# One load in place of three for the last rows of W_down, and seven loads in place of five for x, in a decode block

## Chip, core and metric

The kernel runs on one core of one Trainium2 chip. The metric is device time in microseconds (us), as the median of several runs. The core has five engines that run side by side and wait for each other on semaphores: PE (TensorE, matrix products), DVE (VectorE), ACT (ScalarE), POOL (GpSimd) and SP (SyncE, which here only issues loads). Sixteen DMA engines bring data from the chip's memory (HBM) into the core's SBUF, 128 partitions of on-chip memory. A load is issued by SP or ACT, is cut into packets that the sixteen engines share out, and tells its end by a semaphore.

## What is computed

One decoding step of a transformer block for two sequences (B = 2), one token each, in bf16: layer norm, attention over a cache of 8192 positions and 32 heads, a residual, a second layer norm, and a gated feed-forward part.

```python
x = A_x                                              # (2, 1, 512)
q = layernorm(x) @ wq                                # 512 -> 32 heads x 128
p = softmax(q . k_cache * 128 ** -0.5)               # k_cache, v_cache: (2, 32, 8192, 128)
h = x + (p @ v_cache) @ wo                           # 4096 -> 512
n = layernorm(h)
h2 = h + (relu(n @ W_gate) * (n @ W_up)) @ W_down    # 512 -> 1376 -> 512
```

The two caches make up 256 MiB of the 281 MB that are read; everything else is small beside them.

## The kernel before

**Tiles.** Three buffers of 128 x 32768 bf16 (8 MB each, `bufs[0]` to `bufs[2]`) hold what is streamed from HBM. A step works on four heads of one sequence and needs one K tile and one V tile of 8 MB. There are 15 such steps (0 to 14, `Q` = 14 is the last) and two half steps of two heads each at the end. K and V tiles alternate over the three buffers, so at any time one tile is worked on while others are on their way. Below, K0 is the K tile of step 0, V1 the V tile of step 1, and so on.

**A step.** `products` (line 375) multiplies the K tile by the repeated q on VectorE, in place; `scores` (lines 393 to 399) sums the products by halving and ends in `scol`, the scores. A part of the columns goes through PE instead (`scores_pe`). Then come the largest score, the exponentials on ACT, and `values` (line 446), where PE multiplies them with the V tile. A K buffer is free when `scores` has ended on VectorE, and a V buffer when `values` has ended on PE; the next tile for the buffer is issued by SP (`load_tile`, line 165) once these have told it so. The order on every engine is the order of the program text, written out by hand.

**The head.** ACT issues x (line 190) in five pieces, one row at a time: 512 B, 512 B, 512 B, 256 B and 256 B. SP issues wq (line 193, 4 MB), K0 and V0. x, wq and the row form of q share the third buffer, so K1, which is to go there, waits until q has been made. From x follow its transposition (lines 238 and 239), the layer norm (`ln_cols`), q (line 252), its spreading over the partitions (lines 259 to 271), its transposition (line 275) and the copies `qTs` (line 276), after which VectorE begins step 0.

**The tail.** When attention nears its end, SP issues wo in pieces, then W_gate and W_up (line 612) and W_down (lines 616 and 621). W_down has 1376 rows, which are 10 chunks of 128 and one of 96. The last chunk is kept as 128 partitions that begin 32 rows early, at row 1248 (`FSETS[-1]`), because W_gate and W_up are read in the same 128 columns: partitions 0 to 31 of chunk 10 (`FC - 1`) repeat rows that chunk 9 has. So that they count once, line 616 loads only partitions 32 to 127, as three loads of 32 rows of 1 KB, and line 647 sets the 32 others to zero on VectorE. The other chunks follow in four loads (line 621): chunks 0 to 4, 5 to 7, 8, and 9. The end of the kernel is `g_ps` = n W_gate, `gate` = relu(g) times a factor (line 706), `u_ps` = n W_up, `hm` = gate times u (line 727) in two parts, and `down` (line 719), which takes chunks 0 to 4, then chunk 10, then 5 to 9. The sums are copied to `yrow` (lines 734 and 735), and line 736 writes it out.

**Completion semaphores.** The loads of SP and ACT share eight completion semaphores, given out in turn in the order of the program text. A load waits until the load eight places before it, which had the same semaphore, is complete. In the built program before, x has numbers 0 to 4, wq 5, K0 6, V0 7, and none of these waits; K1 is the next with number 0. At the tail, the three small loads of W_down wait for the V tile of the last half step and for two pieces of wo, the following ones for further pieces of wo, the last one (chunk 9) for W_gate, and the write of the result for W_up.

Of the kernel before, what the change touches and what calls it, by code (L numbers as in the profile page):

```python
# [13 lines left out]
def _free(t, offset, dims):  # L14

    return bass.AP(tensor=t.tensor, offset=t.offset + offset, ap=[t.ap[0]] + [list(d) for d in dims])


def _dram(t, offset, dims):
    return bass.AP(tensor=t.tensor, offset=t.offset + offset, ap=[list(d) for d in dims])  # L20
# [3 lines left out]
def kernel(  # L24
# [13 lines left out]
    nc = tc.nc  # L38
    P = nc.NUM_PARTITIONS
    B, Sq, D = A_x.shape  # L40
    _, Hkv, Sk, Dh = A_k_cache.shape
    Hq = A_wq.shape[1] // Dh
    F = B_W_gate.shape[1]
# [29 lines left out]
    FSETS = [(0, 5), (5 * P, 3), (8 * P, 1), (9 * P, 1), (F - P, 1)]  # L73
    FC = 11
    AGAIN = 32
# [51 lines left out]
    wd_sb = bufs[1][:, 0:FC * D].rearrange("p (c n) -> p c n", c=FC)  # L127
# [58 lines left out]

    with tc.manual_schedule():

        for b, k, n in ((0, 0, 2), (0, 2, 2), (1, 0, 2), (1, 2, 1), (1, 3, 1)):
            nc.scalar.dma_start(  # L190
                out=xr[b:b + 1, k * P:(k + n) * P], in_=_dram(A_x, b * D + k * P, [[D, 1], [1, n * P]]),
            )
# [9 lines left out]
            out=nscale, in_=nscale, compare_op=ALU.not_equal, fill=-SCALE,  # L202
# [5 lines left out]
            out=ident_f, in_=ident_f, compare_op=ALU.not_equal, fill=1.0,  # L208
# [4 lines left out]
            out=sel, in_=sel, compare_op=ALU.not_equal, fill=1.0,  # L213
# [9 lines left out]
            out=pick, in_=pick, compare_op=ALU.not_equal, fill=1.0,  # L223
# [24 lines left out]
        for g0 in range(0, NQ, 4):  # L248
            for n0 in range(NH * g0 * Dh, NH * (g0 + 4) * Dh, 4 * Dh):
                q_ps = ps2.tile([B, 4 * Dh], f32, tag="o")  # L250
                for c in range(KC):
                    nc.tensor.matmul(  # L252
                        out=q_ps, lhsT=xn[:, c, :], rhs=wq_sb[:, c, n0:n0 + 4 * Dh], start=(c == 0), stop=(c == KC - 1),
                    )
                nc.vector.tensor_copy(qrow[:, n0:n0 + 4 * Dh], q_ps)
            for b in range(B):
                r_ps = ps2.tile([P, 4, Dh], f32, tag="tp")
                for j in range(NH):
                    nc.tensor.matmul(
                        out=r_ps[j * (P // NH):(j + 1) * (P // NH)], lhsT=sel[:, b, 0:P // NH],  # L260
# [5 lines left out]
        for j in range(2):  # L266
            nc.tensor.matmul(
                out=r_ps[j * (P // 2):(j + 1) * (P // 2)], lhsT=sel[:, B - 1, :],
# [38 lines left out]
        def sums(i):  # L307

            _, _, n, z = heads(i)
            z_ps[i] = ps.tile([P, n], f32, tag="mx", name="z_ps")  # L310
            nc.tensor.matmul(out=z_ps[i], lhsT=ones, rhs=z, start=True, stop=True)
# [175 lines left out]
        def lay_rows(k, sps, scalar=False):  # L487

            r = SROWS[k]
            or_ps = ps.tile([P, B, r], f32, tag="mx")  # L490
            for b in range(B):
                nc.tensor.matmul(out=or_ps[:, b, :], lhsT=sps[b], rhs=rest[r], start=True, stop=True)
            if scalar:
                nc.scalar.activation(out=orow[k], in_=or_ps.rearrange("p b c -> p c b"), func=ACT.Copy)
            else:
                nc.vector.tensor_copy(orow[k], or_ps.rearrange("p b c -> p c b"))
# [90 lines left out]
        for k in range(1, len(SETS)):  # L587
# [3 lines left out]
            out=wo[:, (HM + 1) * D:Hq * D], in_=_dram(A_wo, (HM + 1) * Dh * D, [[P // 4 * D, 4], [D, P // 4], [1, D]]),  # L591
# [19 lines left out]
        for w, src in ((0, B_W_gate), (1, B_W_up)):  # L611
            nc.sync.dma_start(
                out=wgu[:, w].rearrange("p c f -> p (c f)"), in_=_dram(src, 0, [[KC * F, P], [1, KC * F]]),
            )
        for q0 in range(AGAIN, P, AGAIN):
            nc.sync.dma_start(
                out=wd_sb[q0:q0 + AGAIN, FC - 1, :], in_=_dram(B_W_down, (F - P + q0) * D, [[D, AGAIN], [1, D]]),
            )
        for f0, n in FSETS[:-1]:
            fc = f0 // P  # L620
            nc.sync.dma_start(out=wd_sb[:, fc:fc + n, :], in_=_dram(B_W_down, f0 * D, [[n * D, P], [1, n * D]]))
        late = bufs[1][:, HALF + D:HALF + D + P + D]
        hrow, parts3 = late[0:3 * B, 0:D], late[0:3 * B, D:D + B]
# [6 lines left out]
            out=z2_ps, lhsT=ones, rhs=_free(zc, ((B - 1) * NQ + groups[Q][1]) * NH, [[1, nb]]), start=True, stop=True,  # L630
# [13 lines left out]
        values_cols(p1, 0, half)  # L644
        for k in range(1, len(SETS)):
            lay_rows(k, sps[k - 1])
        nc.vector.memset(wd_sb[0:AGAIN, FC - 1, :], 0.0)
        sums(Q + 2)
        shares(Q + 2)
        values_cols(p1, half, p1.nt)  # L650
# [43 lines left out]
        for c in range(KC):  # L694
            nc.tensor.transpose(hT_ps[:, c, :], hb[:, c].rearrange("p k b -> p (k b)"), ident)
        nc.scalar.activation(
            out=hrow.rearrange("q (p c) -> q p c", c=KC), in_=hT_ps.rearrange("q c p -> q p c"), func=ACT.Copy,
# [7 lines left out]
        gate = small.tile([P, FC, B], f32, tag="gate")  # L705
        nc.vector.scalar_tensor_tensor(
            out=gate, in0=g_ps, scalar=0.0, in1=_free(rvar, 0, [[0, FC], [1, B]]), op0=ALU.max, op1=ALU.mult,
        )
        parts = [(range(0, UP), "of", ps), (range(UP, FC), "tp", ps2)]
        u_ps = [pool.tile([P, len(part), B], f32, tag=tag, name="u_ps") for part, tag, pool in parts]  # L710
        SIDE = P // KC
# [55 lines left out]
```

## Time and profile before

| | |
|---|---|
| runs, median (lowest to highest) | 659.28 us (658.91 to 659.56, 3 runs) |
| the profiled execution: span from the first to the last instruction | 657.5 us |
| HBM read, rate over the span | 281.05 MB, 427 GB/s |
| busy: VectorE, PE, ACT, POOL | 85%, 54%, 19%, 4% |
| mean granted TensorE clock | 0.76 |
| chain that ended last: DMA, VectorE, PE | 37%, 42%, 18% |
| the loads of x in that chain | 2.0% |
| VectorE idle before line 375, waiting for a K tile | 44.9 us in 13 waits |

The page of a profile sums up one execution. Its chain follows the work that ended last back to the start, at each step to what released it. A timeline lists instructions by their start, with the length, the engine, the line, what is written and read, and in brackets the time that the engine was idle before and what ended that. SPq and ACTq are the issues of loads by SP and ACT. Windows give the busy time of each engine in a stretch of time. An engine that is busy is not for that reason the one that sets the time: VectorE is busy for 85% of the span and still waits for K tiles.

### The profile page before, as it was taken

How to read it: one execution, taken by the hardware profiler on the slowest of the kernel's cores; microseconds unless marked ns; L12 is line 12 of the kernel's file. 1: busy time of each engine (PE TensorE's matmuls, PEld its weight loads, DVE VectorE, ACT ScalarE, POOL GpSimd, SP SyncE). 2: the span in 40 equal slices, each digit the busy share in tenths (PEclk: the TensorE clock that was granted, in tenths of full speed). 3: DMA queues.
4: the chain of work that ended last, by engine and by line, in shares of the span. 5: the costliest groups of instructions: out<-in, count | busy, mean ns of one | idle time of the engine just before them, and what ended most of it. 6: DMA issues, size and time to landing. Idle time of an engine off the chain costs nothing.

```text
span 657.5 us, 5117 instructions
## 1 busy us (share of the span) xinstructions
PE 352.1 (54%) x2118; PEld 158.9 (24%) x2118; DVE 558.1 (85%) x252; ACT 123.6 (19%) x337; POOL 24.1 (4%) x36
## 2 busy tenths in 40 slices
PE   0730934809175380926539092552918458291997
PEld 0310311304022130312204031220403224030456
DVE  0599697988979799897979989796997969999982
ACT  0230030200203020030301103030210304201870
POOL 3080000000000000000000000000000000000020
PEclk9975775958778596877959687695968869686895
DMA  9999999999999999999999999999999999999997
GB/s 383 447 444 447 387 440 443 447 399 444 439 443 436 419 436 435 439 439 436 423 443 424 439 440 427 447 416 443 439 423 440 423 443 436 423 444 413 425 425 291
DMA packets 6948, 281.37 MB, mean 428 GB/s; under 512 B 809, under 2 KB 1422, under 8 KB 1934
## 3 DMA queue, kind: packets, MB, share of 16 engines
q1 hardware_dynamic: 6916, 281.06, 99.1%
q8 instruction: 16, 0.26, 0.1%
q14 instruction: 6, 0.05, 0.0%
q10 hardware_dynamic: 10, 0.00, 0.0%
HBM read 281.05 MB, written 0.00 MB: 427 GB/s over the span
## 4 chain that ended last, share of the span: by engine, by line
DVE 42%; DMA 37%; PE 18%; ACT 1%; issue 1%; ACTq 0%; SPq 0%; DVEq 0%
DMA tile<-in_A_k_cache_dram 30%; DVE tile L375 19%; DVE tile L393 18%; PE pv_ps L446 16%; DMA tile<-in_A_wo_dram 4%; DVE scol L395 2%; DMA tile<-in_A_x_dram 2%; DMA tile<-in_B_W_down_dram 1%; PE q_ps L252 1%; DVE pgq L420 1%; ACT ecol L415 1%; DVE pm L399 1%; DVE qrep L395 0%; DVE pm L410 0%; DVE hmax L412 0%
## 5 line engine op out<-in xcount | busy, mean ns | idle before, releaser
L446 PE MATMUL pv_ps<-tile,pgq 128*16 128x512 bf16 x960 | 244.3, 421 | 235.8 <-DVE pgq L420 223.2
L375 DVE TENSOR_TENSOR tile<-tile,qrep 128x29696 bf16<-128x29696 bf16 (+3 forms) x16 | 232.4, 14524 | 44.9 <-DMA tile<-in_A_k_cache_dram 44.9
L393 DVE TENSOR_TENSOR tile<-tile 128x14848 bf16<-128x14848 bf16 (+7 forms) x68 | 236.4, 3477 | 2.2
L446 PEld LDWEIGHTS <-pgq 128*16 128x16 bf16 x960 | 91.6, 97 | 378.1 <-DVE pgq L420 234.5
L451 ACT ACTIVATE pv<-pv_ps 16x512 f32<-16x512 f32 (+1 forms) x16 | 9.4, 589 | 243.7 <-PE pv_ps L446 243.6
L350 ACT ACTIVATE tile<-t_ps 128x1024 bf16<-128x1024 bf16 x53 | 52.6, 1022 | 12.6 <-PE t_ps L349 12.1
L415 ACT ACTIVATE ecol<-scol,nmax 128x256 bf16<-128x256 f32 x14 | 7.1, 508 | 196.1 <-DVE nmax L414 196.1
L340 PE MATMUL row_ps<-tile,qz 128*24 128x512 bf16 (+1 forms) x98 | 30.1, 389 | 18.0 <-ACT tile L350 17.9
L349 PE MATMUL t_ps<-ident,tile 128*128 128x128 bf16 x424 | 32.3, 229 | 13.0 <-DMA tile<-in_A_k_cache_dram 13.0
L349 PEld LDWEIGHTS <-tile 128*128 128x128 bf16 x424 | 25.8, 103 | 28.1 <-issue 14.2
L395 DVE TENSOR_REDUCE scol<-tile 128x232 f32<-128x1856 bf16 (+1 forms) x14 | 28.9, 2067 | 0.5
L641 POOL TENSOR_TENSOR tile<-ident 6x2 bf16<-6x2 bf16 x1 | 2.1, 2147 | 583.5 <-ACT tile L381 583.5
L420 DVE TENSOR_TENSOR pgq<-ecol,ownb 128x1024 bf16<-128x1024 bf16 x15 | 10.4, 692 | 10.3 <-ACT ecol L415 10.3
L381 ACT ACTIVATE tile<-tile 128x128 bf16<-128x128 bf16 x60 | 17.6, 293 | 1.9 <-DVE tile L375 1.9
L281 POOL COPY qzp<-qTs 128x4 bf16<-128x4 bf16 x1 | 15.0, 14982 | 26.1 <-DVE qTs L276 26.1
L375 DVE TENSOR_TENSOR tile<-tile,qpair 128x4096 bf16<-128x4096 bf16 (+3 forms) x4 | 15.5, 3883 | 0.0
L340 PEld LDWEIGHTS <-qz 128*24 128x24 bf16 (+1 forms) x98 | 7.9, 92 | 27.6 <-issue 22.7
L239 DVE CAST xc<-x_ps 128x8 f32<-128x8 bf16 x1 | 0.2, 167 | 15.5 <-PE x_ps L238 15.5
L367 ACT ACTIVATE scol<-sc_ps 32x24 f32<-32x24 f32 (+1 forms) x56 | 11.7, 209 | 7.7 <-PE sc_ps L362 7.2
L362 PE MATMUL sc_ps<-ident_f,tile 24*128 24x24 f32 (+2 forms) x68 | 7.2, 220 | 11.1 <-ACT tile L358 11.1
L358 ACT ACTIVATE tile<-row_ps 24x512 f32<-24x512 f32 (+2 forms) x17 | 10.0, 586 | 13.5 <-PE row_ps L340 13.5
L381 ACT ACTIVATION_READ_ACCUMULATOR tile<-tile 128x1 f32 x60 | 11.2, 186 | 0.0
(133 smaller groups left out, 143.8 us busy)
## 6 DMA issues: line engine op xcount, KB each, us to landing
tile<-in_A_k_cache_dram SPq DMA_DIRECT2D x2, 4096.0 KB
tile<-in_A_v_cache_dram SPq DMA_DIRECT2D x2, 4096.0 KB, 19.6
tile<-in_A_wq_dram SPq DMA_DIRECT2D x1, 4096.0 KB, 12.2
tile<-in_A_wo_dram SPq DMA_DIRECT2D x1, 2048.0 KB
tile<-in_B_W_gate_dram SPq DMA_DIRECT2D x1, 1376.0 KB, 22.8
tile<-in_B_W_up_dram SPq DMA_DIRECT2D x1, 1376.0 KB
tile<-in_A_wo_dram SPq DMA_DIRECT2D x1, 1024.0 KB, 23.8
tile<-in_B_W_down_dram SPq DMA_DIRECT2D x1, 640.0 KB
```

What stands on the lines that cost most here:

```text
L281: nc.gpsimd.tensor_copy(qzp[:, :, 6:8], qTs[:, B - 1, Hq - NH:Hq].rearrange("p (k j) -> p k j", j=2),)
L340: nc.tensor.matmul(out=row_ps, lhsT=z, rhs=s.kt[:, (nv + c0 + k) * Dh:(nv + c0 + k + 4) * Dh], start=(u == 0), stop=(u == U - 1),)
L349: nc.tensor.transpose(t_ps[:, k, :], s.kt[:, t * Dh:(t + 1) * Dh], ident)
L350: nc.scalar.activation(out=s.kt[:, (nv + c0) * Dh:(nv + c0 + TPC) * Dh], in_=t_ps.rearrange("p t s -> p (t s)"), func=ACT.Copy,)
L367: nc.scalar.activation(out=scols[s.i][r, nv:s.nt].rearrange("p (u t) -> p t u", t=4), in_=sc_ps[r, :, :, j], func=ACT.Copy,)
L375: nc.vector.tensor_tensor(out=kv, in0=kv, in1=_free(s.qr, 0, [[0, n], [1, Dh]]), op=ALU.mult)
L381: nc.scalar.activation(out=kv, in_=kv, func=ACT.Copy, accum_out=scols[s.i][:, t:t + 1])
L393: nc.vector.tensor_tensor(out=lo, in0=lo, in1=hi, op=ALU.add)
L395: nc.vector.tensor_reduce(out=scol[:, s.na:s.nv], in_=_free(s.kt, s.na * Dh, [[Dh, s.nv - s.na], [1, 8]]), axis=AXIS.X, op=ALU.add,)
L415: nc.scalar.activation(out=ecol, in_=scols[s.i], func=ACT.Exp, scale=SCALE, bias=nmax, accum_out=zs[:, s.b, s.g:s.g + 1],)
L420: nc.vector.tensor_tensor(out=s.pg, in0=_free(ecol, 0, [[VG, s.nt // VG], [0, NH], [1, VG]]), in1=_free(ownb, 0, [[0, s.nt // VG], [VG, NH ...
L446: nc.tensor.matmul(out=pv_ps[s.i][r, :], lhsT=s.pg[:, u].rearrange("p j t -> p (j t)"), rhs=s.vt[:, u * VG * Dh:(u + 1) * VG * Dh], start= ...
```

## The change

W_down's last chunk is loaded whole, all 128 partitions with one load, so that partitions 0 to 31 hold rows 1248 to 1279 a second time; this load goes ahead of the four others, where the three small ones stood. The zeroing of these partitions of W_down on VectorE goes, and the same 32 partitions of `gate` are zeroed for chunk 10 after `gate` is made, so that `hm` is zero there. x comes in seven loads: 512 B and six times 256 B.

```diff
-        for b, k, n in ((0, 0, 2), (0, 2, 2), (1, 0, 2), (1, 2, 1), (1, 3, 1)):
+        for b, k, n in ((0, 0, 2), (0, 2, 1), (0, 3, 1), (1, 0, 1), (1, 1, 1), (1, 2, 1), (1, 3, 1)):
             nc.scalar.dma_start(
                 out=xr[b:b + 1, k * P:(k + n) * P], in_=_dram(A_x, b * D + k * P, [[D, 1], [1, n * P]]),
             )
...
-        for q0 in range(AGAIN, P, AGAIN):
-            nc.sync.dma_start(
-                out=wd_sb[q0:q0 + AGAIN, FC - 1, :], in_=_dram(B_W_down, (F - P + q0) * D, [[D, AGAIN], [1, D]]),
-            )
-        for f0, n in FSETS[:-1]:
-            fc = f0 // P
+        for f0, n in FSETS[-1:] + FSETS[:-1]:
+            fc = min(-(-f0 // P), FC - 1)
             nc.sync.dma_start(out=wd_sb[:, fc:fc + n, :], in_=_dram(B_W_down, f0 * D, [[n * D, P], [1, n * D]]))
...
-        nc.vector.memset(wd_sb[0:AGAIN, FC - 1, :], 0.0)
...
+        nc.vector.memset(gate[0:AGAIN, FC - 1, :], 0.0)
```

The number of transfers is the same, 56 with the write of the result. Between x and W_down each load has a semaphore two places further on: x has 0 to 6, wq 7, K0 0 and V0 1. In the built program K0 therefore waits for the first load of x and V0 for the second.

## The prediction

> **What bounds the kernel now.** I read the page first (busy shares, slices, queues), then the chain that ended last, then SyncE's and VectorE's timelines, then the last microseconds in windows.
>
> ```profile
> DMA  9999999999999999999999999999999999999997
> ...
> q1 hardware_dynamic: 6916, 281.06, 99.1%
> ...
> q10 hardware_dynamic: 10, 0.00, 0.0%
> ```
>
> The DMA engines work in every slice but the last. Queue q1 (SyncE's loads) holds 99.1% of the time of 16 engines; so a microsecond in which the engines have nothing to fetch is a microsecond lost, and a computation counts only if it makes a load late. Queue q10 holds the five loads of x: ten packets, two a load.
>
> In the chain of waits (start, length, what):
>
> ```profile
> 2.11 12.96 DMA tile<-in_A_x_dram
> 15.07 0.14 issue
> ...
> 30.63 0.31 PE r_ps L267 x2
> 30.96 41.50 DMA tile<-in_A_k_cache_dram
> 72.48 15.64 DVE tile L375
> ```
>
> x, 2 KB, lands only at 15.07 us, and the whole making of q hangs on it until the third tile load (K of step 1) goes out at 30.96. SyncE's issues (start, length):
>
> ```profile
> 0.74 0.39 SPq L193 DMA_DIRECT2D tile<-in_A_wq_dram  x1
> 1.19 0.41 SPq L165 DMA_DIRECT2D tile<-in_A_k_cache_dram  x1
> 1.66 0.42 SPq L165 DMA_DIRECT2D tile<-in_A_v_cache_dram  x1
> 30.96 0.33 SPq L165 DMA_DIRECT2D tile<-in_A_k_cache_dram  x1
> 64.47 0.33 SPq L165 DMA_DIRECT2D tile<-in_A_v_cache_dram  x1
> 83.93 0.33 SPq L165 DMA_DIRECT2D tile<-in_A_k_cache_dram  x1
> ```
>
> Wq, K0 and V0 go out at once; V1 (64.47) waits for VectorE to finish step 0's scores, which free K0's buffer, and K2 (83.93) for PE's values of step 0. VectorE's timeline:
>
> ```profile
> 32.31 0.19 DVE L276 COPY qTs<-qT_ps 128x32 bf16<-128x32 bf16 x1 [0.35 <-PE qT_ps L275]
> 32.41 15.08 DVE L375 TENSOR_TENSOR tile<-tile,qrep 128x28672 bf16<-128x28672 bf16 x1
> ...
> 62.30 2.02 DVE L395 TENSOR_REDUCE scol<-tile 128x224 f32<-128x1792 bf16 x1
> ...
> 72.48 15.62 DVE L375 TENSOR_TENSOR tile<-tile,qrep 128x29696 bf16<-128x29696 bf16 x1 [5.49 <-DMA tile<-in_A_k_cache_dram]
> ```
>
> Step 0's products begin 0.10 us after q is ready, without idle time, and step 0 runs through to the end of scol; after step 0 VectorE idles 5.49 us. So a later q moves V1's issue one for one, and what counts is how far ahead of need V1 is issued.
>
> **The change, part by part.** *x by seven loads.* The page does not say where x's 13 us go; the trace's records of single packets on q10 do:
>
> ```
> load   data at   bytes   completion at
> x0      1.64      512        1.66
> x1      6.17      512        7.40
> x2      8.62      512        9.85
> x3     11.07      256       12.29
> x4     12.30      256       14.73
> ```
>
> All of x goes through one engine (the spacing shows it). There each of x1's to x4's packets, the 4-byte completion too, waits for its turn behind one packet of q1: 1.22 us apart while these are Wq's 32 KB rows, 2.43 us for the last, behind a 64 KB row of K0 (2.42 us in q1's records). x0 alone went through before Wq's first packet (1.78). Two more loads are four more packets, all after Wq's end (its completions lie at 12.00 to 12.62) and within K0's (31.32 to 31.94): 4 x 2.43 = 9.7 us. x lands at 24.8. ACT's two more issues (0.21 to 0.27 us each) lie under this.
>
> What follows at the other stations: K1 needs q's matmuls done and goes out at 40.7 rather than 30.96. V0's packets last until 50.7, so nothing is lost. VectorE starts step 0 at 42.1 and V1 goes out at 74.2. K1's packets end at 70.16 to 70.52 on fifteen engines and at 72.00 on one. After an issue into an empty queue Wq's first packets began 1.04 to 1.84 us later; I take that for V1: 75.2 to 76.0. The gap is 4.7 us (75.2 less 70.52) to 5.9 us (76.0 less 70.16), on the engine that lags 3.2 to 4.0. I take the middle, 5.3, since completions at the end spread over several lagging engines and one early lag less will not shorten it. K2 then goes out at 93.6, 19.46 us after V1 as now; V1's transfer takes 8 x 2.42 = 19.35: another 0.1. Step 1 starts at 76.7 rather than 72.48, so V2 goes out at 109.9, still 3 us ahead of K2's end (93.6 + 1.0 + 19.4 = 114); step 2 again waits for its K, and no further gap opens. Nothing gives the 5.4 us back: the engines are full from there on.
>
> The Trainium skill ("DMA: Bandwidth & Descriptors", section "Queues, rings and completion order") says that each engine takes turns between queues by whole packets, which may hold several descriptors. The turns agree with the table; that a load's data and completion would share one turn does not, as they lie 1.23 us apart. By one turn a load the sum would be that of the first rival.
>
> *Completion semaphores.* Eight serve all loads in turn, so two more in front move every load by two places until W_down's two fewer. In the built program K0 now waits for x0, V0 for x1. x0 is complete at 1.66: K0 goes out near 1.8 instead of 1.19, and Wq covers that until 12. V0 goes out at 7.5, under K0 until 31.3. Cost 0; the cover is gone for K0 if x0 lands after about 11. Behind K0's wait on SyncE stand V0 and K1, behind V0's only K1. In the steady part a load waits for the one eight before it, landed long ago.
>
> *W_down's last chunk.* One load instead of three: 32 rows more of 1 KB, two per engine at 46 ns (q1's records), less two completions at 9 ns: +0.07. Two issues less on SyncE (0.31 to 0.34 us each), and the last W_down load, which waits now for the gate weights (2.6 us on SyncE), will wait for a W_o load that landed near 641. The windows (time, then busy time and count for five engines, granted clock, DMA share, GB/s) say whether that helps:
>
> ```profile
> 650.00:651.00 1.00, 1.00 (x6) 0.72 (x6) 0.00 (x0) 0.45 (x1) 0.00 (x0) 0.50 0.98 375
> 651.00:652.00 1.00, 0.70 (x18) 0.67 (x18) 0.69 (x4) 0.13 (x1) 0.00 (x0) 0.50 0.72 279
> 652.00:653.00 1.00, 1.00 (x35) 0.91 (x33) 0.21 (x2) 0.00 (x0) 0.00 (x0) 0.50 0.65 248
> 653.00:654.00 1.00, 0.91 (x32) 0.67 (x29) 0.12 (x1) 0.00 (x0) 0.00 (x0) 0.50 0.45 165
> ```
>
> The engines are full until 651 and then run out one by one with work issued by 648; an earlier issue puts nothing ahead of the bytes already queued. I take 0; the gain is at most the empty share, 0.28 + 0.35 + 0.55 = 1.2 us.
>
> *The zeroing.* The memset of W_down's 32 rows (0.27 us on VectorE, in idle time) goes. One of gate comes, nearest in size to the 0.17 us of its neighbours. It stands before the product with u, for which VectorE idles 0.44 us waiting on PE: 0, and 0.17 without that cover.
>
> **Sum.** 5.3 + 0.1 + 0.07 = +5.5 us. The profiled span goes from 657.5 to 663.0. The runs' median, 659.28, lies 1.8 above this span, and I carry that over: 664.8 us, with its own bounds at 662.7 (3.2 + 0.1 + 0.07, if the lagging engine decides the end) and 665.5 (5.9 + 0.1 + 0.07 + 0.17).
>
> **Rivals.**
> 1. One turn for each x load. x then lands two turns later, 4.9 us; V1 goes out at 69.3, its packets start at 70.4 to 71.2, and the gap is about 0.5: 659.9. Against it stand four pairs in the table; for it, only that shorter data might behave otherwise. 7%.
> 2. Not slower: K0, now behind a wait, comes to the engines so late that x passes between the end of Wq and K0's first row. x would then be in by 13, q would wait for nothing, and step 0 would start on K0's landing as now: 659.3 + 0.1 = 659.4. It decides only if x0 completes after about 10; it completes at 1.66. 3%.
> 3. x0 loses its place, which it has by 0.12 us ahead of Wq's first row. Then all seven queue up, six more turns than now: 6 x 2.43 = 14.6, x at 29.7, V1 out at 79.0, gap 10.2: 669.6. The runs shown lie within 0.65 us of each other, so it has not happened there. 5%.
> 4. Faster: the head is hidden after all and the earlier W_down issue buys its bound: 659.28 - 1.2 = 658.1. V1's slack speaks against it: K1's end at 70.2 less 64.47 less 1.04 is 4.7, and 9.7 are asked. 3%.
>
> **How the numbers follow.** 82% for the forecast, 18% for the rivals. A measurement of this kernel tells 0.2% (1.3 us) from no change. The forecast and rival 3 are slower: 0.87, and rivals 1, 2 and 4 lie within 0.2% but for a rest: same 0.11, faster 0.02. The range goes from 661.5 (a gap of only 2, for instance if q's matmuls run quicker or V1's start-up is shorter) to 667.0 (q later by another 2 us through a lower granted clock, which was 1.00 there).
>
> **What would show it.** In the profile after: x landing at 24 to 25.5 in the chain; K0 issued near 1.8 and V0 near 7.5; step 0's products starting near 42; V1 issued near 74; a DMA share well below 1 around 71 to 76 and nowhere else before 650; idle VectorE before step 1 gone; the tail as now, 5 us later. x landing before 20 or V1 issued before 70 would make the prediction wrong at its first step; a gap with the end unmoved, at its claim that nothing is given back.

## The result and the profile after

The change makes the kernel slower: 666.36 us (median of 4 runs, 664.96 to 667.74) against 659.42 us before (658.91 to 659.79), a ratio of 1.0105 with a 95% interval of 1.0092 to 1.0118, or +6.9 us. The profiled execution is the longest of the four (667.74 us, span 666.0), so its span lies 8.5 above that of before; where it matters below, a second profile of the same kernel (span 665.2) and the medians stand beside it.

The page of the changed kernel, the same rows as before:

```profile
DMA  9999699999999999999999999999999999999996
...
q1 hardware_dynamic: 6916, 281.09, 98.0%
...
q10 hardware_dynamic: 14, 0.00, 0.0%
```

The fifth slice (66.6 to 83.3 us) has fallen from 9 to 6: the engines ran dry there, and nowhere else before the end. Queue q1 moved almost the same bytes and its share fell by the time in which nothing ran. Queue q10 has its 14 packets, two for each of seven loads.

Its chain of waits (start, length, what):

```profile
2.79 22.19 DMA tile<-in_A_x_dram
24.98 0.14 issue
```

x lands at 24.98 us instead of 15.07. SyncE's issues:

```profile
0.74 0.40 SPq L193 DMA_DIRECT2D tile<-in_A_wq_dram  x1
1.98 0.33 SPq L165 DMA_DIRECT2D tile<-in_A_k_cache_dram  x1
13.04 0.33 SPq L165 DMA_DIRECT2D tile<-in_A_v_cache_dram  x1
41.81 0.33 SPq L165 DMA_DIRECT2D tile<-in_A_k_cache_dram  x1
75.22 0.33 SPq L165 DMA_DIRECT2D tile<-in_A_v_cache_dram  x1
93.58 0.33 SPq L165 DMA_DIRECT2D tile<-in_A_k_cache_dram  x1
```

VectorE's timeline of the same kernel:

```profile
43.06 0.19 DVE L276 COPY qTs<-qT_ps 128x32 bf16<-128x32 bf16 x1 [0.25 <-PE qT_ps L275]
43.17 15.08 DVE L375 TENSOR_TENSOR tile<-tile,qrep 128x28672 bf16<-128x28672 bf16 x1
...
73.05 2.02 DVE L395 TENSOR_REDUCE scol<-tile 128x224 f32<-128x1792 bf16 x1
...
77.66 15.62 DVE L375 TENSOR_TENSOR tile<-tile,qrep 128x29696 bf16<-128x29696 bf16 x1
```

Step 0 begins 10.8 us later, right after q as before, takes the same time, and V1 goes out at 75.22 instead of 64.47. The idle time of 5.49 us before step 1 has gone, for step 1 now begins as soon as VectorE is free. What the engines did meanwhile, in the windows around the gap (time, five engines, granted clock, DMA share, GB/s):

```profile
70.00:72.00 2.00, 0.00 (x0) 0.00 (x0) 1.97 (x2) 0.00 (x0) 0.00 (x0) 0.50 0.08 33
72.00:74.00 2.00, 0.00 (x0) 0.00 (x0) 1.97 (x2) 0.00 (x0) 0.00 (x0) 0.50 0.00 0
74.00:76.00 2.00, 0.00 (x0) 0.00 (x0) 1.83 (x4) 0.00 (x0) 0.00 (x0) 0.50 0.00 0
76.00:78.00 2.00, 0.21 (x1) 0.10 (x2) 1.17 (x4) 0.60 (x2) 0.00 (x0) 0.50 1.53 524
```

From 70.7 to 76.2 us nothing is fetched, but for one engine that ends its last packet of K1 at 72.6; in the kernel before the same four windows carry 492 to 524 GB/s. (A share above 1 counts packets of 64 KB, which last 2.4 us, in the window in which they began.) VectorE is busy all the while: it is still on step 0, the step whose end lets V1 go.

### The profile page after: what moved, and what is told of

Its sections match the earlier page's. It is cut to its first block, busy times and chain, and to the rows that moved or that the text cites. A ratio compares the mean times of both kernels' runs of the same rounds, so it can differ in the third digit from the quotient of the medians.

```text
span 666.0 us, 5117 instructions
## 1 busy us (share of the span) xinstructions
PE 350.0 (53%) x2118; PEld 157.7 (24%) x2118; DVE 557.8 (84%) x252; ACT 123.6 (19%) x337; POOL 23.7 (4%) x36
## 4 chain that ended last, share of the span: by engine, by line
DVE 47%; DMA 32%; PE 18%; ACT 1%; issue 1%; ACTq 0%; SPq 0%; DVEq 0%
DMA tile<-in_A_k_cache_dram 24%; DVE tile L375 21%; DVE tile L393 20%; PE pv_ps L446 16%; DMA tile<-in_A_wo_dram 4%; DMA tile<-in_A_x_dram 3%; DVE scol L395 2%; DMA tile<-in_B_W_down_dram 2%; PE q_ps L252 1%; DVE pgq L420 1%; ACT ecol L415 1%; DVE pm L399 1%; DVE qrep L395 0%; DVE pm L410 0%; ACTq L190 0%
## 5 line engine op out<-in xcount | busy, mean ns | idle before, releaser
L349 PE MATMUL t_ps<-ident,tile 128*128 128x128 bf16 x424 | 30.7, 222 | 12.2 <-DMA tile<-in_A_k_cache_dram 12.1
L349 PEld LDWEIGHTS <-tile 128*128 128x128 bf16 x424 | 24.4, 99 | 26.5 <-issue 13.7
```

The costliest lines, as they stand in the source:

```text
L349: nc.tensor.transpose(t_ps[:, k, :], s.kt[:, t * Dh:(t + 1) * Dh], ident)
```

## The experiments

Times are medians in us, and moments are from the profiled execution. The ratio is against runs of the kernel before on the same chip (medians 659.2 to 659.3), with its 95% interval.

| kernel | x in | V1 issued | time | ratio (interval) |
|---|---|---|---|---|
| before | 15.07 | 64.47 | 659.2 | |
| `wd1_only`: only W_down's part | 15.04 | 64.47 | 659.21 | 1.0001 (0.9992 to 1.0010) |
| `x7_only`: only x's part | 24.92 | 74.46 | 666.03 | 1.0103 (1.0087 to 1.0118) |
| `x5_plus2`: x by five, two idle loads | 15.02 | 64.65 | 659.17 | 0.9998 (0.9989 to 1.0007) |
| `x6`: x by six | 19.99 | 69.68 | 661.09 | 1.0025 (1.0015 to 1.0035) |
| `after_again`: the change | 24.85 | 75.08 | 665.61 | 1.0098 (1.0085 to 1.0112) |
| `k0_four`: the change, K0 in four loads | 15.70 | 65.21 | 659.61 | 1.0006 (0.9997 to 1.0014) |
| `k0_two`: the change, K0 in two loads | 18.50 | 67.95 | 659.76 | 1.0009 (1.0000 to 1.0018) |
| `k0_after_x`: the change, K0 held until x is in | 13.38 | 67.60 | 662.60 | 1.0049 (1.0036 to 1.0062) |
| `x8`: x by eight | 13.67 | 67.29 | 661.90 | 1.0044 (1.0030 to 1.0057) |
| `x1`: x by one load of two rows | 2.04 (last packet) | 64.32 | 659.37 | 1.0005 (0.9996 to 1.0014) |
| `x7_warm`: the change, idle matmuls before x | 24.63 | 74.83 | 665.83 | 1.0098 (1.0083 to 1.0114) |
| `x7_warm2`: and in the layer norm | 25.08 | 73.97 | 663.84 | 1.0068 (1.0054 to 1.0082) |

**The theory** is that of the prediction: x's packets take turns with big rows on one DMA engine, q is late, V1 is issued late, and the engines run dry. **Its rivals**: the tail (W_down's larger load, its place, the zeroing), and the shift of the completion semaphores, which makes K0 and V0 wait.

### One half at a time

```diff
# wd1_only: after, with before's five loads of x
-        for b, k, n in ((0, 0, 2), (0, 2, 1), (0, 3, 1), (1, 0, 1), (1, 1, 1), (1, 2, 1), (1, 3, 1)):
+        for b, k, n in ((0, 0, 2), (0, 2, 2), (1, 0, 2), (1, 2, 1), (1, 3, 1)):
# x7_only: before, with after's seven loads of x
-        for b, k, n in ((0, 0, 2), (0, 2, 2), (1, 0, 2), (1, 2, 1), (1, 3, 1)):
+        for b, k, n in ((0, 0, 2), (0, 2, 1), (0, 3, 1), (1, 0, 1), (1, 1, 1), (1, 2, 1), (1, 3, 1)):
```

> W_down's last chunk by one load and gate zeroed, x by five loads as before. If the loss comes from x's turns on its DMA engine: as before, 659.4 us within 1, x landing at 15.1 us, V1 issued near 64.5. If it comes from the tail (one larger load, its place ahead of the others, the memset on gate): near 666.

> x by seven loads, W_down's last chunk by three loads and its memset as before. By x's turns: as with the whole change, 665 to 668, x landing near 25, V1 issued near 75, DMA engines idle from about 70.5 to 76. By the tail: 659.4.

W_down's part alone leaves the time where it was (1.0001), and x's part alone costs all of it (1.0103 against 1.0105). The tail is out as a cause, and one load in place of three is worth nothing here.

### Seven loads, but x in the first five

```diff
# x5_plus2: after, with before's five loads of x, and behind them
+        spare = bufs[2][0:1, HALF + Hq * Dh + D:HALF + Hq * Dh + D + 2 * P]
+        for k in range(2):
+            nc.scalar.dma_start(out=spare[:, k * P:(k + 1) * P], in_=_dram(A_x, k * P, [[D, 1], [1, P]]))
```

> The whole change, but x comes by its five loads, and two more loads of 256 B follow them that nobody reads. Every later load has the completion semaphore that it has with the change, and K0 and V0 wait as they do there. By x's turns: x is in at 15.1, the two idle loads take the turns up to 25, and the time is as before, 659.4 within 1.3. If the shift of the semaphores (K0 and V0 held back) is the cost: near 666.

SyncE's issues in this kernel:

```profile
1.98 0.33 SPq L165 DMA_DIRECT2D tile<-in_A_k_cache_dram  x1
13.22 0.33 SPq L165 DMA_DIRECT2D tile<-in_A_v_cache_dram  x1
31.12 0.33 SPq L165 DMA_DIRECT2D tile<-in_A_k_cache_dram  x1
64.65 0.33 SPq L165 DMA_DIRECT2D tile<-in_A_v_cache_dram  x1
```

K0 and V0 wait as they do after the change, and seven loads pass on ACT's queue, but x itself is in at 15.02 and the time is that of before. So neither the number of loads nor the later issue of K0 and V0 costs anything; what costs is x standing at the end of the line.

### The length of a turn

```diff
# k0_four (k0_two: pieces=2): after, with
-        load_tile(A_k_cache, steps[0], steps[0].kt)
+        load_tile(A_k_cache, steps[0], steps[0].kt, pieces=4)
# k0_after_x: after, with, ahead of K0's load
+        nc.vector.tensor_copy(bufs[0][0:B, 0:1], xr[:, 3 * P:3 * P + 1])
```

> The whole change (x by seven loads), with K0 in four loads whose rows are 16 KB instead of 64 KB. By x's turns: after Wq each turn takes about 0.61 us (the 16 KB packets in the trace of before) instead of 2.43, so x lands at 12.5 + 5 x 0.61 + 0.3 = 15.9, V1 is issued near 65.5, the engines never run dry, and the time is 659.4 within 1. If the number of x loads costs in another way than by the length of a turn: near 666.

> The whole change, K0 in two loads with rows of 32 KB, so a turn behind a row of K0 is 1.22 us. By x's turns: x lands at 12.5 + 5 x 1.22 + 0.3 = 18.9, V1 is issued at 68.3 to 69.0, 1.0 us before the engines would run dry (K1's end at 70.2 less 1.0 of start-up): 659.2 to 660. If the loss grows with x's landing from 15 on, without a threshold: (18.9 - 15.1) / 9.8 of 6.9, 662.

> The whole change, with K0 held back until all of x has landed (a copy of two of its numbers on VectorE into K0's place, before K0 is loaded there). By x's turns: with no row of K0 to wait for, x is in at about 13, K0 is issued at 13.1 and begins 14.1 to 15.0, after Wq's end at 12.1 to 12.7: one gap of 2.0 us, up to 0.7 more for slow first packets, and none later, since step 0 starts on K0's landing at 34 to 35: 661.2 to 662.3. If seven loads of x cost what the change cost whatever stands behind them: 666 or more (the gap on top: 668).

The records of single packets on q10, for the start of x's last four completions (us):

```
after        12.51   14.95   19.80   24.64     behind rows of 64 KB
k0_two       12.05   13.29   15.72   18.16     behind rows of 32 KB
k0_four      12.27   12.90   14.13   15.37     behind rows of 16 KB
k0_after_x   12.33   12.36   12.38   12.40     nothing behind Wq
```

Same seven loads, same bytes: from the second in each row on, the completions of one load and the next lie two turns apart, 4.85, 2.43, 1.24 and 0.02 us, in proportion to the row that each packet waits behind. From the first to the second it is one long turn only: the data of that load went in behind Wq's own 4-byte completion, which is a packet of q1 as well (in the changed kernel x's completion at 12.507, Wq's at 12.512, x's data at 12.518). With K0 in four loads the time is that of before within the interval, while in `k0_two` x is 3.4 us later than before and costs at most 0.2%: up to a point a later x is free, which speaks for the threshold and against a cost that grows with x's landing from the start. (The pieces of K0 behind the first wait for wq's semaphore until about 13 us in both kernels; the rows of the first piece cover that, and the engines stay busy.) In `k0_after_x` x is early, and the gap lies instead between Wq's end and K0's first rows. Its windows:

```profile
13.00:14.00 1.00, 0.26 (x4) 0.21 (x4) 0.31 (x2) 0.00 (x0) 0.00 (x0) 1.00 0.00 0
14.00:15.00 1.00, 0.59 (x2) 0.50 (x2) 0.30 (x2) 0.00 (x0) 0.00 (x0) 1.00 2.40 786
```

It came out 0.3 above the top of what was expected, at +3.3 us, because K0 was issued at 13.65 and not at 13.1.

### More loads and fewer

```diff
# x6
+        for b, k, n in ((0, 0, 2), (0, 2, 2), (1, 0, 1), (1, 1, 1), (1, 2, 1), (1, 3, 1)):
# x8
+        for b, k, n in ((0, 0, 1), (0, 1, 1), (0, 2, 1), (0, 3, 1), (1, 0, 1), (1, 1, 1), (1, 2, 1), (1, 3, 1)):
# x1
+        nc.scalar.dma_start(out=xr, in_=_dram(A_x, 0, [[D, B], [1, D]]))
```

> The whole change with x by six loads instead of seven. By x's turns: x lands at 15.07 + 2 x 2.43 + 0.2 = 20.1, step 0 starts at 37.4 to 38.3 (17.3 us after x as before, or 18.2 as with the change), V1 is issued at 69.5 to 70.3, just as K1's packets end (70.2 to 70.6); the gap is 0.5 to 1.4 us and up to 0.7 more for slow first packets: 660 to 661.5. If each added load costs the same: 659.4 + 6.9 / 2 = 662.9.

> The whole change with x by eight loads of 256 B. By x's turns: one more load is two more turns behind rows of K0, 4.86 us; x lands near 29.8, V1 is issued at 79.3 to 80.1, the engines run dry for 9.9 to 10.7 us and the first packets are 0.7 slow: about 4.9 more than the change, 670.3 to 671.5. If the loss were bounded, or the engines made part of it good later: below 669.

> The whole change with x by one load of two rows. By x's turns: x is in before 3 us and q by 20, but step 0 still waits for K0's landing at 32, V1 is issued near 64.4, and the time is as before, 659.3 within 1: an earlier x is worth nothing, only a later one costs. If x's landing sets the time one for one: 13 us less, 646.

`x6` is where the theory puts it: of the two added loads the first costs 1.9 us and the second 5, so they do not cost the same. `x1` shows the other side of the threshold: q is ready at 26.9, and yet V1 goes out at 64.32, since step 0 waits for K0.

`x8` is a miss, by about 9 us. SyncE's first loads in it:

```profile
0.74 0.40 SPq L193 DMA_DIRECT2D tile<-in_A_wq_dram  x1
12.97 0.33 SPq L165 DMA_DIRECT2D tile<-in_A_k_cache_dram  x1
13.35 0.42 SPq L165 DMA_DIRECT2D tile<-in_A_v_cache_dram  x1
```

The semaphores are not given out as the text ahead says. The waits show it: in the changed kernel V0 waits for wq (10.7 us) and not for x's second load. That fits if the first load of x has number 0 and wq number 1, and x's others begin at 2. With eight loads of x it is K0 that gets wq's semaphore and waits for the whole of wq, 12 us. Then no row of K0 stands in x's way, x is in at 13.67, and the one gap is K0's own, as in `k0_after_x`. The expectation had counted turns and left out the semaphore; the turns themselves are confirmed by it (x's completions after Wq's end lie 0.02 us apart there too). So the kernel with eight loads is faster than the one with seven.

### PE at q

```diff
# x7_warm: after, ahead of the transposition of x (x7_warm2: 91, and 2, 3 and 5 more before m_ps, v_ps and the first q_ps)
+        busy = ps2.tile([B, 4 * Dh], f32, tag="o", name="busy")
+        for _ in range(84):
+            nc.tensor.matmul(out=busy, lhsT=ident[:, 0:B], rhs=_free(ident, 0, [[0, 4], [1, P]]), start=True, stop=True)
```

> The whole change, with 84 matrix products that nobody reads on PE ahead of the transposition of x, to keep PE busy until x lands. In the changed kernel q's first 16 matmuls took 6.17 us, most at 0.43 us, and the next 16 took 3.62. If that slow start of PE adds to the gap: 3.4 to 3.7 us for the first 16, V1 issued 2.5 us earlier, and the time 663.5 to 664.5. If PE is slow again after the layer norm, or q's length does not set the gap: 666.

> As x7_warm, with 91 idle matrix products before x and 2, 3 and 5 more in the pauses of the layer norm, so that PE has no long pause before q. If PE is fast in q then: q's first 16 matmuls take 3.5 to 3.8 us instead of 6.1 to 6.5, the idle ones cost up to 0.5, V1 is issued at 72.6 to 73.2, the engines run dry for 3.2 to 3.8 us, and the time is 2 us less than the change: 663.3 to 664.3. If the gap does not follow q's length, 665.5 to 666.5.

q's first 16 matmuls on PE's timelines, of the changed kernel and then of `x7_warm2`:

```profile
28.48 6.15 PE L252 MATMUL q_ps<-tile,xn 128*2 128x512 bf16 x16 [0.99 <-DVE xn L185]
```

```profile
28.38 1.89 PE L263 MATMUL q_ps<-tile,xn 128*2 128x512 bf16 x8
30.68 1.89 PE L263 MATMUL q_ps<-tile,xn 128*2 128x512 bf16 x8 [0.41 <-DVE tile L266]
```

In `x7_warm` the idle matmuls ended 2.25 us before PE began on x, and the layer norm followed; q's first 16 took 6.54 us, and nothing was gained. With the pauses filled as well they end at 32.57 instead of 34.63, K1 goes out 1.9 to 2.1 us earlier than in the two profiles of the change and V1 1.1 to 1.3, and the time falls from 665.6 to 663.84. So q's length counts in the gap. The time came as expected, the way to it did not quite: V1 was expected at 72.6 to 73.2 and went out at 73.97, and the engines were dry for 4.52 us and not for 3.2 to 3.8. q's first 16 matmuls took 4.19 us where 3.5 to 3.8 were expected, and later the transposition of q took 1.87 us on PE (1.05 in the changed kernel), with a granted clock of 0.50 from 40 to 42 us, where the changed kernel has 1.00.

The slow start can be read in the granted clock where the trace has records of it. Those of `x7_warm` begin at 6.36 us, and in its windows the clock (third number from the end) is 0.50 while q's matmuls lie 0.43 us apart and 1.00 when they lie 0.22 apart:

```profile
28.00:30.00 2.00, 2.00 (x6) 0.63 (x5) 1.78 (x8) 0.76 (x2) 0.00 (x0) 0.50 1.16 500
34.00:36.00 2.00, 1.23 (x13) 0.38 (x12) 0.68 (x1) 0.54 (x2) 0.00 (x0) 1.00 0.98 426
```

The trace of the changed kernel has no record of the clock before 33.65 us. Up to there its windows print 1.00 all the same, although q's matmuls lie 0.43 us apart; from that moment on they lie 0.22 apart. The Trainium skill ("TensorE: Matmul & The Clock Gate", section "Part 1: The HAM clock gate") has PE start at half rate and go to full rate after some 3.4 us of steady work, in windows that run freely; the factor of two agrees with these durations, and the free windows would fit that the same 16 matmuls took 5.21, 5.46, 6.15 and 6.14 us in four profiles.

## Why the prediction came out, and what it missed

The prediction of 664.8 us, slower, held in sign, in place and in cause; the measured +6.9 us lies above its +5.5. That it came so near is in part luck, for errors in the terms of the gap partly cancelled.

- **x's turns.** Forecast 24.8, measured 24.98, and shown by `k0_two`, `k0_four`, `k0_after_x` and `x8`, where the row ahead of each packet changed and the spacing of x's packets with it. Rival 1 (one turn for each load) is out: the data and the completion of a load lie one turn apart in every kernel with seven loads.
- **K0 and V0 held back: 0.** Right in the cost (`x5_plus2`), and K0 went out at 1.98 for 1.8. V0 went out at 13.04, not 7.5: it waits for wq, not for x1. K0's rows covered that until 31. Rival 2 (K0 comes so late that x passes) did not happen with seven loads, and is what happens with eight, where K0 waits for wq and not for x0; it was priced without the gap that it opens itself and without slow first packets, 2.7 us in all. Rival 3 (x0 loses its place) did not happen: its completion stands at 1.67.
- **The start of step 0 and V1's issue: mis-sized.** Forecast 42.1 and 74.2, measured 43.17 and 75.22 (43.03 and 75.08 in the second profile). x landed 0.18 us late, and the rest is PE. The step took the start of q from the trace of before unchanged, including the moment at which PE becomes fast, and read the granted clock there as 1.00. That trace has no record of the clock before 21.70 us, and until then q's matmuls lie 0.43 us apart, for 3.1 us from the start of q at 18.56; in the changed kernel it is 5.2 us (28.48 to 33.65). This was a matter of the run: in `x7_only` it is 3.8 us (28.41 to 32.17), and V1 goes out at 74.46.
- **The gap: right, but a term was missing.** Forecast 5.3 us; from the packet records the engines were dry for 5.82 us on average (5.81 in the second profile, 5.08 in `x7_only`). V1's later issue alone would have made it 6.3. Two other sizes took 0.5 back: V1's first packets began 1.18 us after the issue on average, not 1.44 as the middle of the forecast has it, and K1's packets ended at 70.58 on average, the lagging engine counted, not at 70.34. Not in the sum at all: the first 16 packets after the gap took 3.07 us on average and not 2.42, another 0.65.
- **K2 and later loads.** The forecast 0.1 did not come, for PE finished step 0's values a little sooner (K2 issued 18.36 us after V1 instead of 19.46; it is 17.90 in `wd1_only`, so this is a matter of the run). No further gap opened on all engines at once, and nothing was given back; VectorE waits for its K tiles in steps 2 and on as before.
- **W_down, its earlier issue, and the zeroing: 0.** `wd1_only` is at 1.0001. In the changed kernel the memset of gate lies in VectorE's wait for u, as this part of its timeline shows, and takes 0.06 us where 0.17 was assumed; rival 4 has nothing left.

```profile
660.01 0.06 DVE L704 MEMSET gate<- 32x2 f32 x1
660.60 0.17 DVE L723 TENSOR_TENSOR hm<-gate,u_ps 128x10 bf16<-128x10 f32 x1 [0.54 <-PE u_ps L681]
```

The expectation for `after_again` was that its span exceeds 657.5 by the gap plus 0.7 us. That makes 664.0, and the span is 665.2, so a part of the loss lies elsewhere. The gap and the slow restart together, from the packet records, against the growth of each profiled span over 657.5:

```
            dry   slow first packets   sum    span
x6          0.63        0.52           1.15   +1.0
x8          1.71        0.78           2.49   +2.2
k0_after_x  2.51        0.67           3.18   +3.4
x7_warm2    4.52        0.72           5.24   +5.3
x7_only     5.08        0.63           5.71   +6.4
x7_warm     5.56        0.62           6.18   +6.4
after 2nd   5.81        0.68           6.49   +7.7
after       5.82        0.65           6.47   +8.5
```

("Dry" is the time around the gap in which an engine had no packet of q1, as a mean over sixteen; the next column is the excess of the first sixteen packets of 64 KB over 2.42 us, also as a mean.) The two terms account for all but 0.7 us in the first six. In the two profiles of the changed kernel itself 1.2 and 2.0 us are left. There more of the later 64 KB packets took longer than 2.42 us; their excess after 80 us, 1.36 and 1.57 us an engine against 0.73 before and 0.82 in `x7_only`, makes up 0.6 to 0.8 of it. Most of the rest is idle time of the engines beyond the gap: 0.7 us more than before after 640 us in both (0.6 in `x7_only`, which is nearly all of what is left there; kernels without a gap have up to 0.4 more than before), and 0.1 and 0.6 us more in short pauses of single engines between 80 and 640. Why the later packets are slower in these two runs and not in `x7_only`, which has the same head, was not found; it goes with the wider spread of the changed kernel's runs.

No version tried beats the kernel before. Those that keep W_down's single load and lose nothing clear of noise are `wd1_only`, `x1`, `x5_plus2` and `k0_four`.

## What to carry to other kernels

Here a small load on a DMA engine that is busy with big rows paid one big row for each of its packets, its completion included (2.43 us behind 64 KB, 0.6 behind 16 KB), so the number of small loads ahead of a needed value and the row size of the load behind them set its latency, and not its bytes. In a kernel that is bound by its loads, ask of a late value how far ahead of need the next big load is issued: up to that slack the delay is free, and beyond it every microsecond is paid, and the restart on top. When loads share completion semaphores in turn, adding one changes who waits for whom, so read the waits of the built program before counting; here the kernel with eight loads of x, which makes K0 wait, is 4 us faster than the one with seven.

## What the hardware showed that was not expected

- After every gap the first 64 KB packets of the sixteen engines were slow: 2.94 to 3.20 us on average against 2.42 in the steady stream, in eight profiles with gaps of 0.6 to 5.8 us. Running dry costs this in addition to the gap.
- In the changed kernel the dry queue restarts 0.96 to 1.89 us after the issue (V1 issued at 75.22, first packets at 76.18 to 77.11), about as the kernel's first load does (1.04 to 1.84).
- How long PE stays slow at q differs from run to run: 3.1, 3.8 and 5.2 us from q's start in `before`, `x7_only` and the changed kernel. With PE kept busy ahead of q it is fast from the first matmul (8 in 1.89 us).
- When nothing else is queued on the engine, the packets of x follow each other at 0.02 us, where they were 2.43 us apart behind rows of 64 KB.
